# Channel attention into a GELU feed-forward: operands of v in 25 small tiles, the seven-product scheme in first steps too, softmax in ten pieces, side work placed by a table

## The chip, the cores and the metric

One core of a Trainium2 chip runs the whole program. The metric is device time in microseconds (us), the median of three runs. Engine names are those of the profile: PE (TensorE matmul), PEld (its weight load), DVE (VectorE), ACT (ScalarE), POOL (GpSimd), SP (SyncE, which issues all DMAs here).

## The reference

```
B, N, C = 4, 6080, 256          # attention over channels, per batch
qn = q / (norm(q, axis=1) + 1e-6);  kn = k / (norm(k, axis=1) + 1e-6)
s  = kn.T @ qn / tau            # 256 x 256 per batch
a  = exp(s - s.max(-1)); a /= a.sum(-1) + 1e-9
x  = v @ a                      # 6080 x 256 per batch
h  = x @ w_in                   # 256 -> 2048
out = (0.5 * h * (1 + erf(h / sqrt(2)))) @ w_out      # 2048 -> 256
```

All is float32.

## The kernel before

The product `a @ w_in` is folded once per batch into weights `wh`/`wl` (function `w_part`, four groups g of 512 hidden columns), so a token needs two products: v with these weights, then the GELU with `w_out`. Every float32 operand stands as a high part and a low part, and a product is three matmuls (`passes`: high·high, high·low, low·high).

The tokens of a batch are cut into six pairs p of blocks (twice 512 tokens, the last twice 480), each pair into eight steps u of 256 hidden units. A step (b, p, u) has *first products* (v by weights) and *second products* (GELU by `w_out`); the second products of a step are issued between the first products of the next one. Both are done by a scheme of seven products for a 2 x 2 block product instead of eight (`strassen`): the first products from the second pair of batch 0 on, the second ones from its third pair on, except in step u=0 of each pair and in the very last step. Where the second products take the scheme, the GELU goes into a tile `x` (`whole`), DVE makes sums of its blocks (`sums`, four pieces), ACT casts their high parts (`gh0`, `gh1`), DVE subtracts for the low parts (`gl0`, `gl1`), and PE runs four products of 512 columns (j=1) and seven of 256 (`work`) into the PSUM banks c00, c01, p0 and p1. Without the scheme PE runs eight of 512. At the end of a pair, `combine` and `merge` put p0, p1, c00 and c01 together on DVE and store.

The first products use two PSUM banks by turns, h0 and h1 (`ring`). The results of the first two products and of the third are copied out by ACT (p1, p5, u2), and three results are added to these by DVE (the operations written `h<-h,u2`, `h<-h,p5`, `h<-h,p1`), so that a bank comes free when its copy or addition ends.

The seven operands of v come from four blocks of a pair, loaded as one tile `v_raw`, four sums `vs0` to `vs3` (`v_sum`), and a high and low part of each (`v_split`: ACT casts `vh`, DVE subtracts `vl`). Each of these names has one buffer, so the split for the next pair overwrites the operand that the last step still reads.

Side work for the next batch runs beside the steps: scores as bursts of matmuls (`burst`; `load_qk` and `split_qk` bring their operands), sums of squares (`norm_part`), the softmax (`softmax`, a generator that is advanced in pieces), and the new weights (`load_win`, `w_part`, `w_split`). `at(step, slot, job)` puts a job into a step: slots 0 to 5 stand behind the first to sixth first product, 6 behind the last second product, 8 and 9 at the end of the step. From pair (0, 1) on every engine works in the order in which the program was written (`InOrder`); before that a scheduler orders the instructions. All records of PE, DVE and ACT carry the line of the helper, L138.

Of the kernel before, what the change touches and what calls it, by code (L numbers as in the profile page):

```python
# [17 lines left out]
P = 128  # L18
# [20 lines left out]

NS = 1024  # L40
# [9 lines left out]
NARROWS = (12, 18)  # L50

# [14 lines left out]
def channel_attention_gelu_ffn(ctx, tc, qk, kqt, vt, tau, w_in, w_out, out):  # L66
# [79 lines left out]

    raws = {}
# [39 lines left out]
    def qk_fill():  # L187
# [9 lines left out]
        acc = state["sacc"] = pm.tile([P, NCT, NT], F32, name="sacc")  # L197
# [21 lines left out]
    def burst(b, k, m):  # L219
# [121 lines left out]
    def softmax(first):  # L341
# [39 lines left out]
        dve.reciprocal(out=r, in_=z)  # L381

# [12 lines left out]
        es = []  # L395
        rden = pm.tile([P, 8], F32, name="rden", bufs=2)
# [5 lines left out]
        if not first:  # L402
            yield
# [11 lines left out]
        eh = pm.tile([P, NCT, C], F32R, name="eh")  # L415
        el = pm.tile([P, NCT, C], F32R, name="el")
# [13 lines left out]
    def w_first(g, m, tmp):  # L430

        if m == 0:
            name = (f"vh{T2}", f"vl{T2}", f"vh{T3}", f"vl{T3}")[g]
            a21s[g] = pv.tile([P, 2, 2, P], F32R, name=name)
# [19 lines left out]
    def w_part(b, g, m):  # L454
# [56 lines left out]
    def v_blocks(b, p):  # L511
        n = PAIRS[p][1]
        raw = vraw[b, p]
        return {(k, j): raw[:, k, j * n:(j + 1) * n] for k in range(2) for j in range(2)}

    def v_sum(b, p, i):
        n = PAIRS[p][1]
        x = v_blocks(b, p)
        if i == 0:
            vts[b, p] = [pv.tile([P, NT], F32, name=f"vs{k}") for k in range(4)]  # L520
        ts = [t[:, :n] for t in vts[b, p]]
        to, x0, x1 = ((0, x[0, 1], x[0, 0]), (2, x[1, 1], x[0, 1]), (1, x[1, 1], ts[0]), (3, x[1, 0], ts[1]))[i]
        dve.tensor_tensor(out=ts[to], in0=x0, in1=x1, op=ALU.subtract)

    def v_split(b, p, i):
        n = PAIRS[p][1]
        x = v_blocks(b, p)
        src = {B11: x[0, 0], B21: x[1, 0], B22: x[1, 1]}.get(i)
        if (b, p) == (0, 0) and i == B12:
            src = x[0, 1]  # L530
        if src is None:
            src = vts[b, p][i - T1][:, :n]
# [4 lines left out]
        yield  # L537
        dve.tensor_tensor(out=lo[:, :n], in0=src, in1=f32(hi[:, :n]), op=ALU.subtract)


# [14 lines left out]
    def strassen(b, p, u):  # L555
        return u > 0 and (b, p) > (0, 1) and (b, p, u) != (B - 1, NP - 1, NU - 1)
# [54 lines left out]
    def first_products(b, p, u):  # L611
# [51 lines left out]
    def plain_products(b, p, u):  # L663
# [9 lines left out]
        for j in (1, 0):  # L673
            for i in (1, 0):
# [7 lines left out]
                flush()  # L682
                if (i, j) != (0, 0):
# [4 lines left out]
    def second_products(b, p, u, blocks):  # L688
# [89 lines left out]
    def merge(b, p, c):  # L778
# [4 lines left out]
        parts = ((0, n // 2), (n // 2, n)) if last and c == NCT - 1 else ((0, n),)  # L783
        for lo, hi in parts:
# [128 lines left out]
    bursts = {}  # L913
    for b in range(1, B):
        start, num, den = (8, 5, 2) if b == 1 else (4, 14, 5)
        for k in range(FIRSTB if b == 1 else 0, NQS // NB):
            bursts[b, k] = (b - 1) * NP * NU + start + k * num // den
# [14 lines left out]
    EDGE = 8  # L932

    for (b, k), s in bursts.items():
        prev = bursts.get((b, k - 1), s - 3)
        for t in range(NB):
            js = k * NB + t
            at(prev - 1 + t, EDGE, lambda b=b, js=js: load_qk(b, js))

            def split(b=b, js=js, step=prev + 1 + t):  # L940
                gen = split_qk(b, js)
                next(gen)
                at(step, 2, lambda: next(gen, None))
            at(prev + 1 + t, 1, split)
        for m in range(NCT):
            at(s + m, EDGE, lambda b=b, k=k, m=m: burst(b, k, m))

        def drop(b=b, k=k):
            for t in range(NB):
                hls.pop((b, k * NB + t))  # L950
        at(s + 1, EDGE, drop)
    for b in range(1, B):
        base = (b - 1) * NP * NU
        for i in range(2 * NCT * NSC):

            def norm(b=b, i=i, step=base + 8 + i):
# [3 lines left out]
                at(step + 1, 2, lambda: next(gen, None))  # L960
            at(base + 8 + i, EDGE, norm)

# [110 lines left out]
```

## Time and profile before

| | |
|---|---|
| median of 3 runs | 2174.79 us (2174.49 to 2175.36) |
| profiled execution | 2174.69 us, its span 2172.9 us |
| PE busy | 2152.8 us, 99% of the span, 11061 matmuls |
| DVE busy | 1734.9 us, 80% |
| ACT busy | 1622.5 us, 75% |
| DMA | 352.18 MB, mean 162 GB/s |

Busy times are unions of the recorded durations of an engine's instructions. Durations of neighbouring matmuls overlap, so the time that one costs is the distance between starts. In a row of the timeline the text in brackets is the idle time of the engine ahead of the instruction and what ended it.

### The profile page before, as it was taken

How to read it: one execution, taken by the hardware profiler on the slowest of the kernel's cores; microseconds unless marked ns; L12 is line 12 of the kernel's file. 1: busy time of each engine (PE TensorE's matmuls, PEld its weight loads, DVE VectorE, ACT ScalarE, POOL GpSimd, SP SyncE). 2: the span in 40 equal slices, each digit the busy share in tenths (PEclk: the TensorE clock that was granted, in tenths of full speed). 3: DMA queues.
4: the chain of work that ended last, by engine and by line, in shares of the span. 5: the costliest groups of instructions: out<-in, count | busy, mean ns of one | idle time of the engine just before them, and what ended most of it. 6: DMA issues, size and time to landing. Idle time of an engine off the chain costs nothing.

```text
span 2172.9 us, 29906 instructions
## 1 busy us (share of the span) xinstructions
PE 2152.8 (99%) x11061; PEld 1822.7 (84%) x11061; DVE 1734.9 (80%) x2732; ACT 1622.5 (75%) x2692; POOL 1.3 (0%) x8
## 2 busy tenths in 40 slices
PE   9999999999999999999999999999999999999999
PEld 8777888887888888888888888888888888888888
DVE  6997788877788788887788878888778777777776
ACT  5767778867777787786777778887677777677675
POOL 0000000000000000000000000000000000000000
PEclk9999999999999999999999999999999999999999
DMA  9545655544344555553434545554344333333332
GB/s 381 180 150 199 213 184 199 183 161 146 136 144 145 176 204 180 199 202 128 140 135 141 173 168 202 184 205 163 106 146 144 118 129 114 127 128 115 125 119 95
DMA packets 100547, 352.18 MB, mean 162 GB/s; under 512 B 10288, under 2 KB 12464, under 8 KB 98352
## 3 DMA queue, kind: packets, MB, share of 16 engines
q1 hardware_dynamic: 100400, 350.27, 46.3%
q8 instruction: 87, 1.43, 0.3%
q14 instruction: 60, 0.49, 0.1%
HBM read 312.74 MB, written 37.49 MB: 161 GB/s over the span
## 4 chain that ended last, share of the span: by engine, by line
PE 87%; DVE 7%; ACT 4%; issue 1%; DMA 0%; DVEq 0%; ACTq 0%; POOL 0%; POOLq 0%
PE h L138 45%; PE c L138 33%; PE p L138 9%; DVE h L138 2%; DVE vl L138 2%; DVE x L138 1%; ACT gh L138 1%; DVE gl L138 1%; ACT x L138 1%; ACT vh L138 1%; ACT g L138 0%; DVE small L138 0%; ACT L138 0%; ACT p L138 0%; DVE osb L138 0%
## 5 line engine op out<-in xcount | busy, mean ns | idle before, releaser
L138 PE MATMUL c<-gh,wo 128*128 128x512 f32 (+3 forms) x2460 | 870.4, 364 | 0.4 <-DVE wo L138 0.4
L138 PE MATMUL h<-vh,wh 128*128 128x512 f32 (+1 forms) x1312 | 520.3, 397 | 12.9 <-DVE h L138 2.8
L138 PEld LDWEIGHTS c<-gh,wo 128*128 128x128 f32 x2460 | 462.2, 188 | 81.9 <-DVE wo L138 1.5
L138 PE MATMUL h<-vh,wl 128*128 128x512 f32 (+1 forms) x1312 | 513.5, 391 | 0.0
L138 PE MATMUL h<-vl,wh 128*128 128x512 f32 (+1 forms) x1312 | 513.5, 391 | 0.0
L138 ACT ACTIVATE gh<-h 128x512 fp32r<-128x512 f32 (+1 forms) x446 | 277.9, 623 | 238.2 <-DVE h L138 219.2
L138 PE MATMUL c<-gl,wo 128*128 128x512 f32 (+3 forms) x1230 | 443.8, 361 | 0.1
L138 DVE TENSOR_TENSOR gl<-x,gh 128x768 fp32r<-128x768 f32 (+3 forms) x306 | 329.8, 1078 | 63.5 <-ACT gh L138 63.3
L138 DVE TENSOR_TENSOR gl<-g,gh 128x512 fp32r<-128x512 f32 (+1 forms) x462 | 314.5, 681 | 49.3 <-ACT g L138 47.1
L138 DVE TENSOR_TENSOR h<-h,p 128x512 f32<-128x512 f32 (+1 forms) x368 | 251.4, 683 | 79.5 <-PE h L138 68.3
L138 ACT COPY p<-h 128x512 f32<-128x512 f32 (+1 forms) x368 | 213.7, 581 | 126.3 <-PE h L138 126.2
L138 PEld LDWEIGHTS h<-vh,wh 128*128 128x128 f32 x1312 | 247.0, 188 | 72.3 <-ACT p L138 9.2
L138 ACT CAST gh<-x 128x768 fp32r<-128x768 f32 (+3 forms) x306 | 286.8, 937 | 16.7 <-DVE x L138 11.7
L138 PEld LDWEIGHTS h<-vh,wl 128*128 128x128 f32 x1312 | 246.4, 188 | 51.9
L138 DVE TENSOR_TENSOR x<-x 128x256 f32<-128x256 f32 (+4 forms) x491 | 241.1, 494 | 52.5 <-ACT x L138 34.8
L138 PEld LDWEIGHTS h<-vl,wh 128*128 128x128 f32 x1312 | 246.7, 188 | 35.4
L138 ACT ACTIVATE g<-h 128x512 f32<-128x512 f32 (+1 forms) x446 | 271.6, 609 | 0.0
L138 PEld LDWEIGHTS c<-gl,wo 128*128 128x128 f32 x1230 | 231.0, 188 | 45.3 <-DVE gl L138 0.5
L138 ACT ACTIVATE x<-h 128x512 f32<-128x512 f32 (+1 forms) x306 | 182.3, 609 | 48.9 <-DVE h L138 47.8
L138 PE MATMUL p<-gh,ws 128*128 128x256 f32 (+1 forms) x918 | 210.2, 280 | 0.0
L138 DVE TENSOR_TENSOR h<-h,u 128x512 f32<-128x512 f32 (+1 forms) x184 | 125.8, 684 | 83.5 <-PE h L138 82.6
L138 PEld LDWEIGHTS p<-gh,ws 128*128 128x128 f32 x918 | 162.6, 189 | 6.8
(153 smaller groups left out, 2229.5 us busy)
## 6 DMA issues: line engine op xcount, KB each, us to landing
wo<-keep_out SPq DMA_DIRECT2D x184, 512.0 KB, 4.5
ws<-keep_sum SPq DMA_DIRECT2D x153, 512.0 KB, 3.7
raw<-qk SPq DMA_DIRECT2D x94, 512.0 KB, 4.5
raw<-kqt SPq DMA_DIRECT2D x72, 512.0 KB, 4.6
v_raw<-vt SPq DMA_DIRECT2D x20, 1024.0 KB, 5.0
out<-osb SPq DMA_DIRECT2D x40, 512.0 KB, 3.9
hl<-keep_in SPq DMA_DIRECT2D x12, 1024.0 KB, 5.4
raw<-w_in SPq DMA_DIRECT2D x8, 512.0 KB, 6.9
```

The source lines that it names most:

```text
L138: r = op(*args, **kw)
```

## The change

- `v` lies in 25 equal tiles v0 to v24 of 512 columns. `take` gives the one that has been free longest, `give` returns a tile at its last use in program order: a raw block or sum when its split is written, an operand when the last step's product has read it. A pair is loaded as four tiles with four DMAs. `eh`, `el` of the first softmax and the plain pair's `a21` come from the same 25; later `eh`, `el` take the buffer of `sacc`.
- The splits of the next pair stand in steps 5, 6, 7 of a pair and in the first step of the next, in place of 7 and the first; the sums in steps 1, 2, 3 and 5 in place of 3 to 6.
- `strassen` holds at u=0 too. The seven products of 256 columns go in another order, p0 first and c00 after p1. `combine` starts at the end of a pair's following first step and `merge` comes in slot 3 of the second one; where all eight steps take the scheme, half of c01 is not written, and the second merge covers half.
- The later softmaxes are advanced in ten pieces, from slot 3 of step 36 of the batch to slot 7 of step 39 (before: seven pieces, from the end of step 36 to the end of step 38), with both scalings ahead of both maxima, and the load of the exponential's table asked for at the end of step 37.
- Steps and slots of all side work come from the table `PLAN`. The bursts of batches 1 to 3 stay 10 or 12; the last `w_split` of a batch comes two steps later.

```diff
+PLAN = {
...
+    "soft": (3, 10, 11, 16, 17, 18, 21, 22, 26, 37),
...
+    "vhi": (52, 54, 66, 71, 72, 73, 81),
+    "vlo": (63, 70, 71, 73, 75, 80, 82),
...
+    room = deque(range(NV))
+    def take(count, dtype=F32R, shape=(P, NT)):
+        got = []
+        for _ in range(count):
+            i = room.popleft()
+            t = pv.tile(list(shape), dtype, name=f"v{i}")
+            owner[id(t)] = i, t
+            got.append(t)
+        return got
+    def give(*tiles):
+        for t in tiles:
+            room.append(owner.pop(id(t))[0])
...
         for m in range(NCT):
             dve.scalar_tensor_tensor(out=ts[m], in0=ts[m], scalar=rk[:, m:m + 1], in1=rq[:, 0:C],
                                            op0=ALU.mult, op1=ALU.mult)
+        if not first:
+            yield
+        for m in range(NCT):
             dve.reduce_max(out=nms[:, m:m + 1], in_=ts[m], axis=AX.X, negate=True)
         yield
         es = []
+        if not first:
+            preload(AF.Exp, x)
+            yield
...
-        raw = pv.tile([P, NCT, 2 * NT], F32, name="v_raw")
-        nc.sync.dma_start(out=raw[:, :, :2 * n],
-                          in_=vt[:, b * N + t0:b * N + t0 + 2 * n].rearrange("(t p) n -> p t n", p=P))
+        raw = {}
+        for k, j in ((0, 0), (1, 0), (1, 1), (0, 1)):
+            x, = take(1, F32)
+            t = b * N + t0 + j * n
+            nc.sync.dma_start(out=x[:, :n], in_=vt[k * P:(k + 1) * P, t:t + n])
+            raw[k, j] = x
...
-        hi = pv.tile([P, NT], F32R, name=f"vh{i}")
-        lo = pv.tile([P, NT], F32R, name=f"vl{i}")
+        hi, = take(1)
+        act.copy(out=hi[:, :n], in_=src[:, :n])
+        yield
+        lo, = take(1)
         vops[b, p, i] = hi, lo
-        act.copy(out=hi[:, :n], in_=src)
-        yield
-        dve.tensor_tensor(out=lo[:, :n], in0=src, in1=f32(hi[:, :n]), op=ALU.subtract)
+        dve.tensor_tensor(out=lo[:, :n], in0=src[:, :n], in1=f32(hi[:, :n]), op=ALU.subtract)
+        give(src)
...
-        return u > 0 and (b, p) > (0, 1) and (b, p, u) != (B - 1, NP - 1, NU - 1)
+        return (b, p) > (0, 1) and (b, p, u) != (B - 1, NP - 1, NU - 1)
...
             product(b, p, u, *ORDER[i], ps, start, stop)
+            if u == NU - 1:
+                give(*vops.pop((b, p, ORDER[i][1])))
...
-        work = (("c00", 1, wpair(0, 0), hb, lb, 2), ("p0", 0, wpair(0, 1), hb, lb, 0),
-                ("c00", 0, (ws[:, 0, 3], ws[:, 1, 3]), hb, lb, 1), ("p1", 0, (ws[:, 0, 0], ws[:, 1, 0]), ht, lt, 0),
-                ("p1", 1, (ws[:, 0, 2], ws[:, 1, 2]), ht, lt, 1), ("p0", 1, (ws[:, 0, 1], ws[:, 1, 1]), ht, lt, 2),
+        work = (("p0", 0, wpair(0, 1), hb, lb, 0), ("p0", 1, (ws[:, 0, 1], ws[:, 1, 1]), ht, lt, 2),
+                ("p1", 0, (ws[:, 0, 0], ws[:, 1, 0]), ht, lt, 0), ("p1", 1, (ws[:, 0, 2], ws[:, 1, 2]), ht, lt, 1),
+                ("c00", 1, wpair(0, 0), hb, lb, 2), ("c00", 0, (ws[:, 0, 3], ws[:, 1, 3]), hb, lb, 1),
                 ("c01", 1, wpair(1, 0), ht, lt, 3))
...
+        if c == NCT - 1 and all(strassen(b, p, u) for u in range(NU)):
+            parts = ((n // 2, n),)
...
-                        spread(gen, step, 1)
+                        spread(gen, step, PLAN["end"][1])
```

The order of instructions at three places. First DVE from the end of step u=0 into u=1 in batch 3, third pair (osb is the pair's output tile, x the GELU tile). Before:

```order
L138 TENSOR_TENSOR gl1_18909<-g_18910,gh1_18908 128x512
L138 TENSOR_TENSOR gl0_18924<-g_18925,gh0_18923 128x512
L138 TENSOR_TENSOR osb_18952<-p0_18271,osb_18952 128x256
L138 TENSOR_TENSOR osb_18952<-p1_18286,osb_18952 128x256
L138 TENSOR_TENSOR osb_18952<-osb_18952,p1_18286 128x256 x2
L138 TENSOR_TENSOR osb_18952<-c00_18175,osb_18952 128x512
L138 TENSOR_TENSOR osb_18952<-c01_18187,osb_18952 128x512
L138 TENSOR_TENSOR h_18982<-h0_18956,u2_18971 128x512
```

After, the same place on DVE:

```order
L171 TENSOR_TENSOR x_19273<-x_19273 128x512
L171 TENSOR_TENSOR x_19273<-x_19273 128x256
L171 TENSOR_TENSOR osb_19305<-p0_18531,osb_19305 128x256
L171 TENSOR_TENSOR osb_19305<-p1_18546,osb_19305 128x256
L171 TENSOR_TENSOR x_19273<-x_19273 128x256
L171 TENSOR_TENSOR gl1_19295<-x_19273,gh1_19294 128x768
L171 TENSOR_TENSOR osb_19305<-osb_19305,p1_18546 128x256 x2
L171 TENSOR_TENSOR gl0_19297<-x_19273,gh0_19296 128x1024
L171 TENSOR_TENSOR h_19354<-h0_19332,u2_19346 128x512
L171 TENSOR_TENSOR osb_19305<-c00_18559,osb_19305 128x512
L171 TENSOR_TENSOR osb_19305<-c01_18566,osb_19305 128x256
```

The sums of x and two wider subtractions take the place of two of 512 columns, the combine operations stand between them, and the merges moved behind the add h.

Second, ACT in step u=0 of the same pair, before (p1, p5, u2 are the copies that free the banks):

```order
L138 COPY p1_18834<-h0_18830 128x512
L138 CAST gh0_18822<-x_18792 128x1024
L138 CAST vh1_18841<-v_raw_18212 128x512
L138 COPY p5_18849<-h1_18845 128x512
L138 CAST vh6_18855<-vs3_18404 128x512
L138 COPY u2_18862<-h0_18830 128x512
```

And after, on ACT:

```order
L171 COPY p1_19202<-h0_19198 128x512
L171 CAST gh0_19188<-x_19163 128x1024
L171 COPY p5_19215<-h1_19211 128x512
L171 CAST v6_19221<-v2_18779 128x512
L171 COPY u2_19226<-h0_19198 128x512
```

One cast of v left this step, and the other one stands behind the copy p5.

Third, ACT at the exponentials of batch 2's softmax, in the fifth pair (t0, t1 are the scores; the table load ahead of gh is the GELU's). Before:

```order
L138 COPY p1_16012<-h1_16008 128x512
L138 CAST gh0_15992<-x_15968 128x1024
L138 COPY p5_16023<-h0_16019 128x512
L138 COPY u2_16032<-h1_16008 128x512
L138 ACT_TABLE_LOAD
L138 ACTIVATE t0_15882,small_15881<-t0_15882,small_15881 128x256
L138 ACTIVATE t1_15884,small_15881<-t1_15884,small_15881 128x256
L138 ACT_TABLE_LOAD
L138 ACTIVATE gh_16045<-h_16043 128x512
```

After, on ACT:

```order
L171 CAST gh1_16306<-x_16279 128x768
L171 ACT_TABLE_LOAD
L171 ACTIVATE junk_16317<-small_16131 128x2
L171 COPY p1_16324<-h1_16320 128x512
L171 CAST gh0_16308<-x_16279 128x1024
L171 COPY p5_16335<-h0_16331 128x512
L171 ACTIVATE t0_16132,small_16131<-t0_16132,small_16131 128x256
L171 COPY u2_16346<-h1_16320 128x512
L171 ACTIVATE t1_16134,small_16131<-t1_16134,small_16131 128x256
L171 ACT_TABLE_LOAD
L171 ACTIVATE gh_16357<-h_16355 128x512
```

The first table load moved to the end of the step before, and the exponentials stand on either side of the copy u2.

More of the change, by code (lines that the diff above doesn't have):

```diff
@@ L38 @@
 NB = 2
+NV = 25
 NS = 1024
@@ L50 @@
 NARROWS = (12, 18)
+PLAN = {
+    "first": {
+        "splits": (10, 10, 13, 14, 15, 16, 18, 19, 20, 21, 23, 24, 25, 26, 28, 29, 30, 31, 33, 34),
+        "loads": (8, 8, 11, 12, 13, 14, 16, 17, 18, 19, 21, 22, 23, 24, 26, 27, 28, 30, 31, 32),
+        "bursts": ((12, 13), (14, 15), (17, 18), (19, 20), (22, 23), (24, 25), (27, 28), (29, 30), (32, 33), (34, 35)),
+        "norms": (9, 10, 11, 12, 13, 14, 15, 16, 17, 19, 20, 21, 22, 23, 25, 26, 27, 28, 29, 30, 31, 32, 33, 34),
+    },
+    "later": {
+        "splits": (2, 3, 5, 6, 7, 8, 10, 11, 13, 14, 16, 17, 19, 20, 21, 22, 24, 26, 27, 28, 30, 31, 33, 34),
+        "loads": (0, 1, 3, 4, 5, 6, 8, 9, 11, 12, 14, 15, 17, 18, 19, 20, 22, 24, 25, 26, 28, 29, 31, 32),
+        "bursts": ((3, 5), (6, 7), (9, 10), (11, 12), (15, 16), (17, 18), (20, 21), (24, 25), (26, 27), (28, 30), (32, 33), (34, 35)),
+        "norms": (2, 3, 4, 5, 6, 7, 9, 10, 11, 12, 13, 14, 16, 17, 18, 19, 20, 21, 22, 23, 25, 26, 27, 29),
+    },
+    "burst": 8,
+    "part": 8,
+    "square": 2,
+    "qhi": 1,
+    "qlo": 2,
+    "start": 36,
+    "soft": (3, 10, 11, 16, 17, 18, 21, 22, 26, 37),
+    "win": (39, 40, 43, 45),
+    "wpart": (41, 43, 45, 47),
+    "wsplit": (42, 44, 46, 50),
+    "wslots": (10, 12, 13, 18, 22, 26),
+    "vload": 0,
+    "vsum": (17, 27, 38, 53),
+    "vhi": (52, 54, 66, 71, 72, 73, 81),
+    "vlo": (63, 70, 71, 73, 75, 80, 82),
+    "end": (8, 10, 13, 13),
+}
 GAPS = (7, 4, 2)
@@ L395, in softmax @@
         es = []
+        if not first:
+            preload(AF.Exp, x)
+            yield
         rden = pm.tile([P, 8], F32, name="rden", bufs=2)
@@ L401, in softmax @@
             es.append(e)
-        if not first:
-            yield
+            if not first:
+                yield
         for m in range(NCT):
@@ L414, in softmax @@
                    identity=ident)
[L415 to L416 removed]
+        if first:
+            eh, el = state["eh"] = take(2)
+        else:
+            keep = pm.tile([P, 2, NT], F32R, name="sacc")
+            eh, el = keep[:, 0], keep[:, 1]
+        eh, el = (x.rearrange("p (d c) -> p d c", d=NCT) for x in (eh, el))
         marks["eh"] = act.copy(out=eh, in_=tpv)
@@ L516, in v_sum @@
     def v_sum(b, p, i):
         n = PAIRS[p][1]
[L518 to L523, printed above, removed]
+        x = vraw[b, p]
+        ts = vts.setdefault((b, p), {})
+        to, x0, x1 = ((T1, x[0, 1], x[0, 0]), (T2, x[1, 1], ts.get(T1)), (T4, x[1, 0], ts.get(T2)),
+                      (T3, x[1, 1], x[0, 1]))[i]
@@ L682, in plain_products @@
                 flush()
+                if u % 2 == 1 and (i, j) == (0, 0):
+                    give(a21)
+                if u == NU - 1 and i == 0:
+                    for x in cols[j]:
+                        give(*vops.pop((b, p, x)))
                 if (i, j) != (0, 0):
@@ L912, in channel_attention_gelu_ffn, with base_soft, plan @@
     FIRSTB = FILL // NB
[L913 to L917, printed above, removed]
+    def base_soft(b):
+        return (b - 1) * NP * NU + PLAN["start"]
+    def plan(b):
+        p = PLAN["first" if b == 1 else "later"]
+        return p["loads"], p["splits"], p["bursts"]
     jobs = {}
@@ L930, in spread, with split, drop, norm @@
             at(step + x // 10, x % 10, lambda: next(gen, None))
[L932 to L951, printed above, removed]
+    EARLY, EDGE = 7, 8
     for b in range(1, B):
         base = (b - 1) * NP * NU
-        for i in range(2 * NCT * NSC):
-            def norm(b=b, i=i, step=base + 8 + i):
+        loads, splits, bursts = plan(b)
+        for k in range(FIRSTB if b == 1 else 0, NQS // NB):
+            r = k - (FIRSTB if b == 1 else 0)
+            for t in range(NB):
+                js = k * NB + t
+                at(base + loads[NB * r + t], EDGE, lambda b=b, js=js: load_qk(b, js))
+                def split(b=b, js=js, step=base + splits[NB * r + t]):
+                    gen = split_qk(b, js)
+                    next(gen)
+                    at(step, PLAN["qlo"], lambda: next(gen, None))
+                at(base + splits[NB * r + t], PLAN["qhi"], split)
+            for m in range(NCT):
+                at(base + bursts[r][m], PLAN["burst"], lambda b=b, k=k, m=m: burst(b, k, m))
+            def drop(b=b, k=k):
+                for t in range(NB):
+                    hls.pop((b, k * NB + t))
+            at(base + bursts[r][1], EDGE + 1, drop)
+        for i, x in enumerate(PLAN["first" if b == 1 else "later"]["norms"]):
+            def norm(b=b, i=i, step=base + x):
                 gen = norm_part(b, *divmod(i, NSC))
```

70 lines of the change are left out of this document (36 added, 34 removed).

## The prediction

> **What bounds the kernel now.** I read the page's busy times first, then the chain, then PE's timeline for the spacing of its matmuls, then windows cut at the starts of steps. On the page (busy share of each engine, the granted clock in 40 slices, the chain's shares):
>
> ```profile
> span 2172.9 us, 29906 instructions
> PE 2152.8 (99%) x11061; PEld 1822.7 (84%) x11061; DVE 1734.9 (80%) x2732; ACT 1622.5 (75%) x2692; POOL 1.3 (0%) x8
> PEclk9999999999999999999999999999999999999999
> PE 87%; DVE 7%; ACT 4%; issue 1%; DMA 0%; DVEq 0%; ACTq 0%; POOL 0%; POOLq 0%
> ```
>
> PE is busy for 99% of the span at full clock and carries 87% of the chain; DMA carries none of it. So a change can win in two ways: fewer matmul columns, or fewer of the gaps in which PE waits for DVE and ACT. The price of a column comes from PE's timeline in an undisturbed step (start, duration, operands):
>
> ```profile
> 1302.84 0.39 PE L138 MATMUL h<-vh,wh 128*128 128x512 f32 x1
> ...
> 1303.53 0.28 PE L138 MATMUL c<-gh,wo 128*128 128x256 f32 x1
> ...
> 1304.23 0.40 PE L138 MATMUL h<-vh,wh 128*128 128x512 f32 x1
> ```
>
> Three 512-column matmuls start within 0.69 us, the six 256-column ones behind them within 0.70. So a trio (the three passes of one product) costs 0.69 us at 512 columns and 0.35 at 256; the printed durations overlap and are no price.
>
> Windows cut at step starts (stretch, length, then busy time of PE, PEld, DVE, ACT, POOL): a plain step of batch 3, a step with a burst, a step u=1, the three softmax steps (u=5 to 7 of the fifth pair) of batches 0 and 2, and u=0 to 2 at the start of batches 1 and 3:
>
> ```profile
> 1872.73:1882.82 10.09, 10.09 (x57) 8.66 (x55) 7.51 (x12) 7.00 (x12) 0.00 (x0) 1.00 0.31 106
> 1352.58:1364.06 11.48, 11.48 (x64) 9.88 (x63) 9.32 (x13) 8.87 (x14) 0.00 (x0) 1.00 0.55 190
> 1852.21:1862.64 10.43, 10.43 (x47) 8.37 (x46) 8.11 (x14) 7.11 (x13) 0.00 (x0) 1.00 0.52 177
> 481.90:517.29 35.39, 32.54 (x170) 26.67 (x169) 28.40 (x60) 25.16 (x43) 0.00 (x0) 1.00 0.24 87
> 1554.19:1589.63 35.44, 32.56 (x171) 26.68 (x169) 28.60 (x61) 25.77 (x44) 0.00 (x0) 1.00 0.25 90
> 604.14:637.70 33.56, 32.95 (x160) 26.68 (x160) 29.48 (x47) 25.80 (x44) 0.00 (x0) 1.00 0.43 151
> 1676.47:1709.73 33.26, 32.66 (x161) 26.68 (x161) 28.45 (x47) 25.46 (x44) 0.00 (x0) 1.00 0.39 139
> ```
>
> The same view over the 19 steps u=0 that follow another pair of their batch (first, last and sum of 19):
>
> ```profile
> 1318.89:1330.63 11.74, 11.74 (x65) 9.77 (x63) 10.69 (x16) 10.90 (x19) 0.00 (x0) 1.00 0.72 250
> ...
> 1841.69:1852.21 10.52, 10.38 (x57) 8.59 (x56) 9.65 (x15) 9.31 (x17) 0.00 (x0) 1.00 0.67 226
> sum 210.84, PE 208.56 PEld 172.50 DVE 191.81 ACT 189.44 POOL 0.00; mean PE 10.98 PEld 9.08 DVE 10.10 ACT 9.97 POOL 0.00
> ```
>
> A plain step has 11 trios of 512 and 7 of 256: 7.59 + 2.45 = 10.04, measured 10.09; a burst adds 1.39. So plain steps hold no wait. From that the waits follow:
> - u=0: seven of the 19 steps are plain in matmuls (10.09), seven hold a burst (11.48), four have products of 480 columns (21 matmuls shorter by 32/512 of 230 ns: 9.79), one has whole second products, 15 trios and a burst (11.76): 201.9 in all. Measured 210.84, so **8.9 us** waited.
> - softmax: three plain steps and six small matmuls (0.7 at 117 ns each) are 31.0; 35.4 measured; **13.3 us** in three batches.
> - batch starts: steps of 9.8 (second products of 480 columns), 10.4 (15 trios) and 10.1, and one w_part group of six matmuls (1.38), are 31.7; measured 33.56, the same in batch 2, and 33.26, so **5.4 us**.
> - u=1: 10.43 against 10.09 is mostly the work counted next; of waiting it holds 0.04 to 0.1, some 1.9 us over 19 steps at most.
>
> **The change part by part.**
>
> *Scheme in the first steps.* At u=0 the four 512-column trios of group j=0 (2.76 us) become seven of 256 (2.46). The 10.43 us step above is where those second products run, and it exceeds the plain step by 0.34, 0.04 of that a wait. 22 pairs, the four of 480 columns a little less: **−6.4 us**. This is work on the bound engine, so nothing can hide it or take it back but a wait. Its other side is on DVE and ACT, by these rows (operation, count, busy, mean ns):
>
> ```profile
> L138 DVE TENSOR_TENSOR gl<-g,gh 128x512 fp32r<-128x512 f32 x388 | 266.0, 686 | 43.1 <-ACT g L138 41.2 <-PE c L138 0.7
> L138 DVE TENSOR_TENSOR gl<-x,gh 128x1024 fp32r<-128x1024 f32 x126 | 154.3, 1225 | 33.8 <-ACT gh L138 33.8
> L138 DVE TENSOR_TENSOR gl<-x,gh 128x768 fp32r<-128x768 f32 x126 | 119.9, 952 | 0.0
> L138 DVE TENSOR_TENSOR x<-x 128x256 f32<-128x256 f32 x252 | 106.4, 422 | 6.4
> L138 DVE TENSOR_TENSOR x<-x 128x512 f32<-128x512 f32 x126 | 87.0, 691 | 34.6 <-ACT x L138 26.4
> L138 ACT ACTIVATE gh<-h 128x512 fp32r<-128x512 f32 x372 | 233.2, 627 | 185.6 <-DVE h L138 170.7 <-PE c L138 13.2
> L138 ACT ACTIVATE x<-h 128x512 f32<-128x512 f32 x252 | 151.6, 613 | 42.2 <-DVE h L138 41.8
> L138 ACT CAST gh<-x 128x1024 fp32r<-128x1024 f32 x126 | 132.6, 1053 | 12.5 <-DVE x L138 11.7
> L138 ACT CAST gh<-x 128x768 fp32r<-128x768 f32 x126 | 105.7, 839 | 3.4
> ```
>
> DVE drops two gl (1.37) and gains 0.69 + 2×0.42 + 0.95 + 1.22 = 3.71: +2.3 us a pair. ACT drops four gelus (2.5) and gains two (1.23) and two casts (1.89): +0.6. The cover is the slack in the step that follows, u=1, where the previous pair's combine and merges now stand among these. In PE's order there, product k of the seven starts at 1.38(k−1) us up to the fifth. DVE starts its sums 0.61 after the seventh product of u=0, which three 256-column trios (1.05) follow, so at −0.44. Its chain to the next add h is 0.69 + 0.42 + two combine ops of 256 columns (0.84) + 0.42 + 0.95 + two more (0.84) + 1.22 = 5.38: it ends at 4.94. The add can begin when the fourth product ends, at 4.83, and takes 0.69: done at 5.63. PE wants that bank for the sixth product at 4.83 + 0.69 + 0.69 + 0.70 = 6.91. So 1.3 us of slack, more where a burst lies ahead: I cost it at **0**, and the 0.1 us a boundary that I leave below covers small misses. The dropped half of the last merge takes 0.27 off DVE. Seconds are reordered so that p0 comes first and c00 after its merge; the lo half of the later blocks is wanted at 6.7, and its producer ends at 4.94.
>
> The 22 extra ws loads and the v loads in four parts add DMA issues on SP, which the chain does not contain:
>
> ```profile
> ws<-keep_sum SPq DMA_DIRECT2D x153, 512.0 KB, 3.7
> ```
>
> A load of 3.7 us has more than a step before its use. The tiles that the v loads overwrite were last read by the fourth and fifth products of the step before, so SP does not block ws or wo behind them: 0.
>
> *Splits spread over u=5 to 8.* The wait at u=0 in the timeline (batch 3; ACT, then the weight load that waited):
>
> ```profile
> 1844.99 0.62 ACT L138 CAST vh<-v_raw 128x512 fp32r<-128x512 f32 x1
> 1845.51 0.58 ACT L138 COPY p<-h 128x512 f32<-128x512 f32 x1
> 1846.15 0.19 PEld L138 LDWEIGHTS h<-vh,wh 128*128 128x128 f32 x1 [0.57 <-ACT p L138]
> ```
>
> A cast of v stands ahead of the copy that frees the bank. The change puts that cast behind the copy, and of seven casts two stand in u=5, one in u=6, three in u=7 and one in u=0 (before: five and two); DVE loses one subtraction at u=0 and reaches its add h 0.69 earlier. I let 1.9 of the 8.9 stay (0.1 each): **−7.0**. u=1 keeps its 1.9.
>
> *Softmax in ten pieces.* The first rows are DVE's, the others ACT's, of batch 0's softmax:
>
> ```profile
> 486.34 0.16 DVE L138 TENSOR_SCALAR small<-small 128x4 int32<-128x4 int32 x1
> ...
> 489.04 0.68 DVE L138 TENSOR_TENSOR h<-h,u 128x512 f32<-128x512 f32 x1
> ...
> 498.90 1.28 ACT L138 ACT_TABLE_LOAD   x1
> 500.20 0.51 ACT L138 ACTIVATE t<-t,small 128x256 f32<-128x256 f32 x1
> ...
> 501.31 1.28 ACT L138 ACT_TABLE_LOAD   x1
> 502.61 0.63 ACT L138 ACTIVATE gh<-h 128x512 fp32r<-128x512 f32 x1
> ```
>
> 2.7 us of small DVE operations stand in front of an add that PE needs, and two table loads with two exponentials (3.7 us) in front of a gelu. After the change the sums of t no longer precede the small operations (two of 0.42 and two small ones, moved to the step before), and these stand ahead of gl0, whose cast DVE used to wait for. From −0.44: sums and gl1 2.48, small ones 2.2, gl0 1.22, diag 0.65, add 0.69: done at 6.8 against 6.91, no wait but no slack. One table load lies under the first product. What stays late: the softmax's four 256-column operations (1.8) now stand ahead of the sums, which end at about 2.9 instead of 1.1; the 1.05 cast follows, then the p5 copy (0.58), at 4.5, where the fourth product wants its bank at 4.14. I take 0.4 for this and 0.6 for the banks of the transposes and of the row sums: 1.0 left a batch, **−10.3**. ACT's second table load is still ahead of a gelu, but that gelu's result is wanted only in the next step.
>
> The Trainium skill (ScalarE: Activation LUTs, What ACT_TABLE_LOAD costs) puts 1283 ns for the load and 1380 for a drain, some 2.66 us for a switch. The trace agrees on the load and shows no drain: the exponential begins 0.02 us after the load's end. By the page the two switches would hold ACT 2.8 us longer in each of three softmaxes, and the sum below would be at most 8 us higher.
>
> *Batch starts.* The last w_split moves two steps later, out of the step that also ends a pair: I let 0.6 of 1.8 stay, **−3.6**. *Pairs 0 and 1* wait some 4 us by the same count (an estimate from plain steps); DVE has the same operations there in another order: **−1** (bounds −2 and +1). *Start:* the first softmax now does both scalings before both maxima, so the first exponential comes up to 0.42 later (a 256-column operation): **+0.3** (bounds 0 and 0.5).
>
> Sum: −6.4 − 7.0 − 10.3 − 3.6 − 1 + 0.3 = −28.0. The profiled execution took 2174.69 us (1.8 beyond its span) and the median of the runs is 2174.79, so the forecast is **2147 us**.
>
> **Rivals.**
> 1. *The waits change places.* The slack of 1.3 us at u=1 is worked out with row means, the softmax's copy is 0.4 late already, and DVE in u=7 and u=0 still has bursts, splits and norms. If half of the 21.9 us of waits that the sum takes away return elsewhere, and each of 22 boundaries waits 0.2 us more, the time is 2146.7 + 11 + 4.4 = 2162. For it: DVE 10.69 of 11.74 us busy in the u=0 row. Against: the after-order has less in that step.
> 2. *DVE becomes the bound at each pair's second step* (the slower side). The 2.3 us of sums and 2.8 of combine and merges share one step. If DVE cannot use its 1.3 us of slack because its inputs come one after the other (combine waits for ACT's copy, gl0 for a cast that waits for the third sum), PE waits for the add. It decides from 1.3 us of wait a boundary (28.0/22); at 2.3, the whole addition uncovered, 2174.7 − 28.0 + 22×2.3 = 2197. Against: bursts of 9.32 us DVE in 11.48 run without any wait.
> 3. *The tiles do not decouple.* If splits wait for tiles that the running step frees, u=0 keeps its 8.9 and the batch starts their 5.4, and the late splits cost as much again at u=1: 2174.7 − 6.4 − 10.3 + 14.3 = 2172. Against: each split takes tiles that an earlier product freed.
> 4. *Narrow matmuls cost more than half.* If each 256-column matmul waited out its 188 ns weight load, a u=0 would cost 21×0.188 = 3.95 against 2.76, 22×1.2 = 26 us more, and the sum would be 2174.7 − 21.6 + 26 = 2179. The rows above (0.70 us for six) exclude nearly all of it.
>
> The Trainium skill (TensorE: Matmul & The Clock Gate, Back-to-back issue gap) gives 131 ns sustained for 512 columns and 81 for 128 in streams of load and matmul; an estimate between them is 98 for 256, by which 21 halves (2.06) cost more than 12 wholes (1.57), and the first term would be +11 us. The trace disagrees: 230 and 117 ns.
>
> **How the numbers follow.** Forecast 0.72 (2138 to 2155: from all the waits counted gone, another 8.5 us, to 8 us less gain), rival 1 0.16, rival 2 0.05, rival 3 0.06, rival 4 0.01. The range 2138 to 2163 takes in the forecast and more than half of rival 1. What a measurement of this kernel can tell is about 0.2%, 4.3 us: forecast and rival 1 are faster, rival 3 is within it or a little faster, rivals 2 and 4 are slower or, in their milder half, level with before: 0.90, 0.05, 0.05.
>
> **What the profile after would show.** Step u=1 at 10.09 us in batch 3 and u=0 at 10.1 to 10.2: the first two terms. Softmax steps in 32 us instead of 35.4. Batch starts within 32 us. A weight load at u=1 that waits for the add h, or u=1 above 10.5, is rival 1 or 2; waits of v casts for PE, or of ws loads, rival 3. The prediction is wrong if the second steps of pairs get longer than they were.

## The result, and the profile after

The changed kernel takes **2142.26 us** (median of six runs, 2141.63 to 2142.51), the kernel before 2174.77 beside it (2174.36 to 2175.36): −32.5 us, ratio 0.985 with a 95% interval of 0.9837 to 0.9862. The profiled execution took 2142.28 us. On the page of the changed kernel (span, busy times, granted clock, chain):

```profile
span 2140.4 us, 30621 instructions
PE 2131.2 (100%) x11259; PEld 1828.8 (85%) x11259; DVE 1768.9 (83%) x2798; ACT 1634.7 (76%) x2695; POOL 1.3 (0%) x8
PEclk9999999999999999999999999999999999999999
PE 92%; DVE 0%; DMA 0%; issue 0%; ACT 0%; DVEq 0%; ACTq 0%
```

DVE and ACT stand at 0% of the chain (7% and 4% before), although both do more work than before. (This chain could be followed back only to 140.9 us of the span, so its shares add up to 93% and leave out the first pair; the one of the kernel before reaches the start.) Windows cut at step starts (stretch, length, then busy time of PE, PEld, DVE, ACT, POOL): a plain step, a u=0 with a burst, a u=1, the softmax of batches 0 and 2, the starts of batches 1 and 3; then the sum of the 19 steps u=0 that stood in the prediction's second view:

```profile
1831.88:1841.97 10.09, 10.09 (x56) 8.66 (x55) 7.51 (x12) 7.00 (x12) 0.00 (x0) 1.00 0.29 106
1298.82:1310.30 11.48, 11.48 (x65) 9.89 (x63) 10.26 (x15) 9.99 (x17) 0.00 (x0) 1.00 0.63 219
1821.78:1831.88 10.10, 10.10 (x56) 8.66 (x55) 9.67 (x18) 7.13 (x13) 0.00 (x0) 1.00 0.44 157
480.83:512.34 31.51, 31.51 (x170) 26.48 (x169) 27.87 (x58) 27.13 (x48) 0.00 (x0) 1.00 0.39 134
1531.56:1563.08 31.52, 31.52 (x170) 26.49 (x169) 27.89 (x58) 27.13 (x48) 0.00 (x0) 1.00 0.39 134
598.36:629.74 31.38, 31.38 (x169) 26.92 (x168) 27.64 (x43) 25.18 (x42) 0.00 (x0) 1.00 0.45 163
1649.08:1680.47 31.39, 31.39 (x169) 26.91 (x168) 26.45 (x42) 23.28 (x39) 0.00 (x0) 1.00 0.36 130
...
sum 202.07, PE 202.07 PEld 174.27 DVE 177.67 ACT 164.56 POOL 0.00; mean PE 10.64 PEld 9.17 DVE 9.35 ACT 8.66 POOL 0.00
```

PE's busy time now equals the length in every one of them: the first steps went from 210.84 to 202.07 us, a softmax from 35.4 to 31.5, a batch start from 33.5 to 31.4, and u=1 from 10.43 to 10.10, the length of a plain step.

Below, PE's waits are counted from its timeline in one way for all kernels: by how much the distance between the starts of two neighbouring matmuls exceeds the undisturbed one (231 ns at 512 columns, 117.5 at 256, 216 at 480, 111.5 at 240; the few other shapes by their own). Over the whole span they fall from 38.4 us to 13.2, and the undisturbed distances themselves add up to 2128.6 before and 2122.1 after. The kernel before ran at 2174.8 to 2175.7 us in the five groups of runs behind this text, so a difference of less than 1 us between kernels of different groups tells nothing.

### The profile page after: what moved, and what is told of

It reads as the page before. It is cut to its first block, busy times and chain, and to the rows that moved or that the text cites. A ratio compares the mean times of both kernels' runs of the same rounds, so it can differ in the third digit from the quotient of the medians.

```text
span 2140.4 us, 30621 instructions
## 1 busy us (share of the span) xinstructions
PE 2131.2 (100%) x11259; PEld 1828.8 (85%) x11259; DVE 1768.9 (83%) x2798; ACT 1634.7 (76%) x2695; POOL 1.3 (0%) x8
## 4 chain that ended last, share of the span: by engine, by line
PE 92%; DVE 0%; DMA 0%; issue 0%; ACT 0%; DVEq 0%; ACTq 0%
PE h L171 47%; PE c L171 33%; PE p L171 12%; DMA wo<-keep_out 0%; DVE x L171 0%; DVE osb L171 0%; DVE hl L171 0%; DVE h L171 0%; ACT g L171 0%; ACT gh L171 0%; DVE v L171 0%; DVE gl L171 0%; DVEq L1143 0%; ACT osb L171 0%; ACTq L171 0%
## 5 line engine op out<-in xcount | busy, mean ns | idle before, releaser
L171 PE MATMUL c<-gh,wo 128*128 128x512 f32 (+3 forms) x2372 | 827.9, 359 | 0.6 <-DVE wo L171 0.6
L171 PE MATMUL h<-v,wh 128*128 128x512 f32 (+1 forms) x2624 | 814.4, 391 | 1.1 <-DVE h L171 1.1
L171 PEld LDWEIGHTS h<-v,wh 128*128 128x128 f32 x2624 | 455.4, 188 | 73.4 <-ACT p L171 2.2
L171 PE MATMUL h<-v,wl 128*128 128x512 f32 (+1 forms) x1312 | 513.4, 391 | 0.0
L171 DVE TENSOR_TENSOR gl<-x,gh 128x768 fp32r<-128x768 f32 (+1 forms) x350 | 376.6, 1076 | 57.4 <-ACT gh L171 57.4
L171 ACT CAST gh<-x 128x768 fp32r<-128x768 f32 (+1 forms) x350 | 327.9, 937 | 46.2 <-DVE x L171 26.9
L171 DVE TENSOR_TENSOR x<-x 128x256 f32<-128x256 f32 (+2 forms) x557 | 274.4, 495 | 80.5 <-ACT x L171 67.5
L171 PEld LDWEIGHTS h<-v,wl 128*128 128x128 f32 x1312 | 246.4, 188 | 52.1
L171 DVE TENSOR_TENSOR h<-h,p 128x512 f32<-128x512 f32 (+1 forms) x368 | 250.8, 682 | 47.7 <-PE h L171 35.4
L171 DVE TENSOR_TENSOR v<-v,v 128x512 fp32r<-128x512 f32 (+3 forms) x257 | 173.9, 677 | 0.5 <-ACT v L171 0.5
L171 PE MATMUL p<-gl,ws 128*128 128x256 f32 (+1 forms) x525 | 146.5, 279 | 0.0
```

Of the source, the lines that this page charges most:

```text
L171: r = op(*args, **kw)
```

## The experiments

### How much room DVE has in the second step

The step u=1 of batch 3 after the change, ACT, DVE and PE (start, duration; in brackets the idle time ahead and what ended it):

```profile
1824.14 1.05 ACT L171 CAST gh<-x 128x1024 fp32r<-128x1024 f32 x1 [0.86 <-DVE x L171]
1825.10 0.57 ACT L171 COPY p<-h 128x512 f32<-128x512 f32 x1
...
1821.56 1.15 DVE L171 TENSOR_TENSOR x<-x 128x512 f32<-128x512 f32 x2 [0.75 <-ACT x L171]
1822.82 0.95 DVE L171 TENSOR_TENSOR osb<-p,osb 128x256 f32<-128x256 f32 x2
1823.69 0.41 DVE L171 TENSOR_TENSOR x<-x 128x256 f32<-128x256 f32 x1
...
1826.90 0.69 DVE L171 TENSOR_TENSOR h<-h,u 128x512 f32<-128x512 f32 x1
...
1825.93 0.63 PE L171 MATMUL h<-v,wh 128*128 128x512 f32 x2
...
1828.72 0.63 PE L171 MATMUL h<-v,wh 128*128 128x512 f32 x2
```

The third add h of the step (`h<-h,u`) ends at 1827.59 and PE wants its bank at 1828.72: 1.1 us of room. But there is a second chain: combine's additions (osb) stand ahead of the third sum of x, ACT's cast waits 0.86 us for that sum, and the copy of the second product stands behind the cast. It ends at 1825.67, and PE takes its bank at 1825.93. To see which of the two sets the time, DVE got three more operations ahead of both:

```diff
+        for _ in range(3 if state.get('u0') else 0):
             tt(out=x[:, 4 * h:6 * h]..., in0=x[:, h:3 * h]..., in1=x[:, 0:h]..., op=ALU.subtract)
```

> The changed kernel with three more 512-column sums on DVE (a repeat of the first sum of x) at the end of each pair's first step, 21 pairs: a test of how much room DVE has in the second step. By the traces the three take 1.8 to 2.1 us, and the slack measured after the change is 1.0 to 1.1 us. Theory (that slack is all there is): PE waits some 0.8 to 1.0 us a pair, 2142.3 + 17 to 22 = 2159 to 2164 us. Rival A (no slack, DVE sets the time there): 21 x 1.9 = 40 us, 2182 us. Rival B (the slack is larger than read, since late work is taken up by later steps): under 5 us, below 2147 us.

Measured 2180.84 us (2178.36 to 2181.68): +38.6, by its size rival A (22 steps carry the sums, not 21). The step in batch 3, and ACT and the weight load in it:

```profile
1853.65:1865.63 11.98, 10.38 (x57) 8.58 (x55) 11.66 (x21) 7.14 (x13) 0.00 (x0) 1.00 0.37 131
...
1857.98 1.04 ACT L171 CAST gh<-x 128x1024 fp32r<-128x1024 f32 x1 [2.84 <-DVE x L171]
1858.93 0.58 ACT L171 COPY p<-h 128x512 f32<-128x512 f32 x1
...
1859.56 0.30 PEld L171 LDWEIGHTS h<-v,wh 128*128 128x128 f32 x2 [2.03 <-ACT p L171]
```

The cast starts 4.33 us after the step's start instead of 2.36, so 1.97 later, and PE waits 1.77 for the copy: the room was **0.2 us**, in ACT's queue and not at the add. The copy's own input was there: the second product starts 1.4 us into the step and takes 0.7. The copy stood behind a cast that waited. The Trainium skill (PSUM — Partial Sum Buffer, Engine vs sequencer instructions) says that the queues of ScalarE and VectorE are strict FIFO; the trace agrees, by these 2.84 us. In 14 of the 22 steps PE waits for this copy (24.2 us in all); in the other eight, which all follow a burst, it waits for DVE's addition of the burst's scores (9.0 us), which the extra sums hold up as well.

Next, combine was moved behind the third sum, with the three sums kept:

```diff
-    "end": (8, 10, 13, 13),
+    "end": (10, 11, 13, 13),
```

> The kernel of the three extra sums, with combine starting one slot later, behind the third of the sums of x and the first low part instead of between them (slots 10, 11, 13, 13). In the extra sums' trace PE waits 1.77 us a pair for the copy of the second product, and that copy stands behind a cast that waits for the third sum, ahead of which combine's first two additions (0.86 us from start to start) stand. Theory (that chain, sum to cast to copy to bank, is what binds; the third add h, with 1.1 us of room, does not yet): the copy comes 0.86 us earlier, PE waits 0.9 a pair, so 2180.8 - 21 x 0.86 = 2163 us. Rival (DVE's total of work in that step binds, whatever its order): it stays at 2180 us.

Measured 2179.72 us: the rival is right. The 1.1 us between the two medians are not to the order's credit: in the profile of the run before, the granted clock is 0.50 in two stretches of 3.4 us (from 264.0 and 1247.1 us), where matmuls of 512 columns start 427 ns apart and PE loses 3.1 us. Without these, PE's waits in the second steps are 36.1 us in that profile and 36.4 in this one. In the step of batch 3 the cast came 0.74 us earlier, but combine's copy moved in between:

```profile
1852.93:1864.61 11.68, 10.54 (x57) 8.69 (x56) 10.94 (x20) 6.56 (x12) 0.00 (x0) 1.00 0.37 135
...
1857.48 0.37 ACT L171 COPY osb<-p 128x256 f32<-128x256 f32 x1
1857.74 0.59 ACT L171 COPY p<-h 128x512 f32<-128x512 f32 x1
```

That gave 0.3 a step. In six steps u=1 with a burst and a splitting it cost 0.6: the wait of 1.0 to 1.2 us for the burst's addition stays, and another of 0.5 comes at the third add h. DVE is nearly full there already without the extra sums, as this window of the changed kernel shows (fourth pair of batch 0):

```profile
347.25:358.73 11.48, 11.48 (x65) 9.89 (x64) 11.20 (x19) 8.86 (x14) 0.00 (x0) 1.00 0.62 214
```

So in these burst steps DVE has hardly any time left (11.20 of 11.48 us busy), and in the others the room is what ACT's queue leaves.

### The scheme in the first steps

The scheme alone, put into the kernel before:

```diff
-        return u > 0 and (b, p) > (0, 1) and (b, p, u) != (B - 1, NP - 1, NU - 1)
+        return (b, p) > (0, 1) and (b, p, u) != (B - 1, NP - 1, NU - 1)
...
+        if c == NCT - 1 and all(strassen(b, p, u) for u in range(NU)):
+            parts = ((n // 2, n),)
```

> The kernel before with one thing alone, the scheme in the first step of each pair too (and the half as long last addition that goes with it); large tiles, places and softmax stay. Theory (the parts add up): 2174.8 - 6.4 = 2168.4 us. Rival (the first step is where DVE is late already, with 8.7 us of PE's waits; the added sums make it later and eat the gain): 2173 to 2180 us.

Measured 2189.95 us (before: 2175.71), ratio 1.0066 (1.0054 to 1.0079): slower by 14.2. PE's waits in the steps u=1 rose from 1.9 to 17.9 us, those at the batch starts from 5.4 to 10.8. The rival is right, and more than it asked (2180 at most): alone, the scheme brings about 20 us of waits and saves 6.4. Of the waits in u=1, 8.9 us stand at the third add h and 7.4 at the first product into c00, whose bank a merge on DVE frees.

The reverse, the scheme taken out of the changed kernel (the first line of the diff turned round):

> The changed kernel, but the first step of each of the 22 pairs of columns computes its products the plain way again (eight second products, no sums). Theory (the scheme is worth its shorter PE time and nothing else, since the waits of these steps are already gone): the changed kernel's 2142.3 plus 22 x 0.29 = 6.4, so 2148.7 us, with PE's waits as they are. Rival (the sums that the scheme adds on DVE load the boundary between pairs, so leaving them out relieves it): part of the 6.4 comes back, 2145 or less; but waits in these steps are already nearly nil, so it should not.

Measured 2173.34 us, +31.1, outside both expectations. PE waits 15.6 us in the steps u=1, 5.4 in the steps u=0 and 3.3 at the batch starts (next to nothing with the scheme). Around the start of one step u=1, at 1846.81, ACT and PE:

```profile
1846.70 0.63 ACT L171 ACTIVATE gh<-h 128x512 fp32r<-128x512 f32 x1 [1.69 <-PE c L171]
1847.24 0.61 ACT L171 ACTIVATE g<-h 128x512 f32<-128x512 f32 x1
1847.76 0.58 ACT L171 ACTIVATE gh<-h 128x512 fp32r<-128x512 f32 x1
1848.24 0.59 ACT L171 ACTIVATE g<-h 128x512 f32<-128x512 f32 x1
...
1848.88 0.72 PE L171 MATMUL h<-v,wh 128*128 128x512 f32 x2 [0.52 <-ACT g L171]
1854.15 0.47 PE L171 MATMUL c<-gh,wo 128*128 128x512 f32 x1 [0.16 <-DVE osb L171]
```

A plain first step writes its last GELUs into the tiles gh1 and gh0, and the products of the step before into c00, which the new order puts near the end, still read gh1. So ACT waits 1.69 us for a product into c, four gelu operations are left to the next step, and the bank that the last of them reads comes free late: 14.1 us of PE's waits stand there. Another 5.9 stand at c00, which without the scheme is wanted as fifth second product, right behind the merges in slot 3. Whether the new order is to blame was tested by undoing both together (old `work`, `"end": (10, 11, 12, 12)`):

> The changed kernel without the scheme in first steps, and with the old order at the end of a pair as well, so that the two are undone together. Theory (the 25 us of waits that came when the scheme alone was taken out are the new order's, which fits only a step with seven narrow products: with the scheme c00 is wanted as ninth product, without it as fifth): those waits go, 2142.3 + 6.4 + up to 2 = 2148 to 2151 us. Rival (the waits come from the scheme's absence itself, since a plain first step hands its GELU over later): it stays near 2173 us.

Measured 2149.36 us, +7.1: the theory, though by the rows above c00 was the smaller part of the waits. Its waits in u=1 are 1.1 us, and the gelu into gh1 starts 1.45 us ahead of the step u=1 instead of 0.11 (third pair of batch 3). And the other way round, scheme and new order together in the kernel before (`work` as in the change, combine from the end of the first step, merges in slot 3 of the second):

> The kernel before with the scheme in first steps and the new order at the end of a pair, large tiles and old places otherwise. Theory (scheme and order belong together, the rest adds up): 2175.7 - 6.4 = 2169 us, perhaps 2 us less since u=1 loses its waits. Rival (casts and subtractions of v still stand in u=0 and make the sums late): u=1 waits as with the scheme alone, 2180 to 2190 us.

Measured 2170.46 us (before: 2174.91), ratio 0.9979 (0.997 to 0.9988): −4.5, near the theory's −6; u=1 waits 1.35 us in place of 17.9, while the batch starts wait 2.4 more than in the kernel before. The last corner, the scheme with the old order in the changed kernel:

> The changed kernel with the end of a pair as it was: c00 first among the seven narrow products, combine from the start of the pair's following second step, both merges ahead of the third add of that step. Theory (the scheme at u=0 is free only because combine starts a step earlier, c00 comes last and the merges stand behind the add): u=1 waits again as it did where the scheme was put alone into the kernel before (19.6 us more in u=1 and the batch starts' second steps), some 2160 us. Rival (the splittings' new places alone make room on DVE): 2142 to 2146 us.

Measured 2156.43 us, +14.2, of it 14.0 of waits in the steps u=1: the theory, at some four fifths of its size. DVE in such a step, and the weight load that waits:

```profile
794.76 1.02 DVE L171 TENSOR_TENSOR osb<-c,osb 128x512 f32<-128x512 f32 x2
795.70 1.22 DVE L171 TENSOR_TENSOR hl<-raw,hl 128x1024 fp32r<-128x1024 f32 x1
796.83 0.68 DVE L171 TENSOR_TENSOR h<-h,u 128x512 f32<-128x512 f32 x1
...
797.57 0.30 PEld L171 LDWEIGHTS h<-v,wh 128*128 128x128 f32 x2 [1.30 <-DVE h L171]
```

The merges (osb from c, 1.02 us) and a splitting stand ahead of the add h. The change puts the merges behind it; the bank c00, which they free, is then wanted later, since c00 stands near the end of `work`. In the changed kernel the four corners are 2142.3 us (scheme, new order), 2156.4 (scheme, old order), 2149.4 (plain, old order) and 2173.3 (plain, new order): the scheme pays only with this order, and the order only with the scheme.

### The places of the splittings

```diff
-    "vhi": (52, 54, 66, 71, 72, 73, 81),
-    "vlo": (63, 70, 71, 73, 75, 80, 82),
+    "vhi": (71, 72, 73, 75, 76, 80, 81),
+    "vlo": (72, 73, 74, 76, 80, 81, 82),
```

> The changed kernel with its 25 small tiles of v, but with the seven splittings of v at the old places, the last two steps of a pair. Theory A (the places are what matters; the tiles only allow them): the waits of the first and second step (8.7 and 1.9 before) come back and the starts of the batches in part, 9 to 14 us, so 2151 to 2156 us. Theory B (giving tiles back one by one is what matters: a splitting no longer waits for a reader of a large tile): nothing comes back, 2142 to 2144 us.

Measured 2163.84 us, +21.6: theory A, and more than it asked. The steps u=0 wait 13.6 us (0.05 with the new places), the first steps of batches 4.0, u=1 0.9. ACT in a u=0 of batch 3, and the weight load:

```profile
1835.00 0.61 ACT L171 CAST v<-v 128x512 fp32r<-128x512 f32 x1
1835.52 0.58 ACT L171 COPY p<-h 128x512 f32<-128x512 f32 x1
...
1836.14 0.30 PEld L171 LDWEIGHTS h<-v,wh 128*128 128x128 f32 x2 [0.56 <-ACT p L171]
```

It is the picture of the kernel before, with 25 small tiles: a cast of v ahead of the copy. In the changed kernel the copy comes first and the cast after it:

```profile
1814.06 0.58 ACT L171 COPY p<-h 128x512 f32<-128x512 f32 x1
1814.54 0.62 ACT L171 CAST v<-v 128x512 fp32r<-128x512 f32 x1
```

So with the tiles and without the places the gain is gone: the places bring it. (The sums of v kept their new places here and were not undone alone.) That the tiles are needed for them follows from the program alone and was not run: with one buffer a name, a split in step 5 would overwrite an operand that steps 5 to 7 still read.

The last `w_split` of a batch back at its old place (`"wsplit": (42, 44, 46, 48)`):

> The changed kernel with the last splitting of a batch's weights back in the step in which a batch begins, two steps earlier. Theory (the prediction's: this move is what took the batch starts' 5.4 us of waits away): 4 us or so come back in three batch starts, 2146 us. Rival (the splittings of v did it: with them alone at their old places the batch starts wait 4.0 us again in their first steps): no wait comes back, 2142 to 2143 us.

Measured 2147.6 us, +5.3: the theory, a little more. But the waits come back elsewhere than they stood before: none in the first step of a batch, 2.2 us in the second, 1.5 in the third, 1.4 in the fourth. In the second step a cast of `w_split` (0.82) stands ahead of ACT's copy of the second product; in the third the subtractions of `w_split` (0.95) and of a splitting (1.22) stand ahead of the add h; in the fourth PE waits for the copy again. The waits in the first steps of batches (4.6 us before) are those of the splittings of v: 4.0 of them came back with their old places.

### The softmax

The seven pieces, places and order of before, without the early table load:

> The changed kernel with the softmax of the later batches as it was: seven pieces at the old places, the two exponentials in one piece, no early load of the tables, each row's scaling and maximum in turn. Theory (the cutting up and the places of the softmax are what took its waits away): the three softmaxes wait 13.4 us on PE again instead of 1.7, so 2142.3 + 11.7 = 2154.0 us. Rival (a part of the softmax's waits went because the sums and the splittings of v no longer fall into the same steps): only about half of it comes back, 2146 to 2150 us.

Measured 2155.57 us, +13.3: the theory. The nine softmax steps wait 14.7 us instead of 1.7. Which of the ten pieces did it: with DVE's cutting kept, and both exponentials together again without the early load,

```diff
-        if not first:
-            preload(AF.Exp, x)
-            yield
...
-            if not first:
-                yield
+        if not first:
+            yield
```

> The changed kernel with both exponentials of a softmax in one piece and without the early load of the exponential's table; the cutting up of DVE's part stays. Theory (ACT's part never made PE wait: in the trace before, PE's waits of a softmax stand at DVE's small operations, at the scalings and maxima and at the transposes, none behind the exponentials): 2142 to 2144 us. Rival (the step terms of the prediction, by which two table loads and two exponentials ahead of a gelu cost as well): 1 to 2 us a softmax, 2145 to 2148 us.

Measured 2144.53 us, +2.3: between the two, nearer the theory. The softmaxes wait 3.6 us, 0.6 each more than with ten pieces, at the end of the step:

```profile
498.60 1.28 ACT L171 ACT_TABLE_LOAD   x1
499.89 0.63 ACT L171 ACTIVATE gh<-h 128x512 fp32r<-128x512 f32 x1
...
502.42 0.30 PEld L171 LDWEIGHTS h<-v,wh 128*128 128x128 f32 x2 [0.47 <-DVE h L171]
```

So of some 4 us that a softmax gained, ACT's part is 0.6. The rest, by difference, belongs to DVE's pieces and their places, which were not undone alone: the small operations, the scalings and the end of the softmax no longer stand as a block ahead of an add.

### What is left

Two of the waits that stand in the trace of the changed kernel, DVE and PE: two splittings of scores' operands in one step of the second pair, and a subtraction behind combine in the last step.

```profile
182.10 2.35 DVE L171 TENSOR_TENSOR hl<-raw,hl 128x1024 fp32r<-128x1024 f32 x2
184.37 0.68 DVE L171 TENSOR_TENSOR h<-h,u 128x512 f32<-128x512 f32 x1
...
185.11 0.30 PEld L171 LDWEIGHTS h<-v,wh 128*128 128x128 f32 x2 [1.37 <-DVE h L171]
...
2133.34 0.72 DVE L171 TENSOR_TENSOR osb<-osb,p 128x240 f32<-128x240 f32 x2
2133.97 0.65 DVE L171 TENSOR_TENSOR gl<-g,gh 128x480 fp32r<-128x480 f32 x1
...
2134.68 0.48 PE L171 MATMUL c<-gl,wo 128*128 128x480 f32 x1 [0.82 <-DVE gl L171]
```

These and two more were to be taken away in one kernel:

```diff
-GAPS = (7, 4, 2)
+GAPS = (7, 5, 2)
...
-        "splits": (10, 10, 13, 14, 15, ...
+        "splits": (10, 11, 13, 14, 15, ...
...
+            if first:
+                dve.reduce_max(out=nms[:, m:m + 1], in_=ts[m], axis=AX.X, negate=True)
...
-            if last and name == "c01" and u < NU - 1:
+            if last and (name, half) == ("p1", 1) and u < NU - 1:
...
-                for i, x in enumerate(PLAN["vsum"]):
+                for i, x in enumerate(PLAN["vsum"] if (b, p) > (0, 0) else (36, 46, 56, 66)):
```

> The changed kernel with the waits that are left in its trace taken one by one: the first two splittings of scores' operands in steps 10 and 11 instead of both in 10 (1.1 us of wait in the third step of the second pair), combine of the last pair right behind the products of p1 (1.0 in the last step), the sums of v for the second pair in the places before (0.8 and 0.5 in the first pair), scaling and maximum of the first softmax row by row again and one matmul more ahead of its transposes (0.75). Theory (these waits are independent): 2142.3 - 3 to 4 = 2138 to 2139 us. Rival (they turn up again at the next thing late, since DVE is 99% busy in the first pair): 2140 to 2142 us.

Measured 2140.44 us (2140.19 to 2141.03), ratio to before 0.984 (0.9827 to 0.9854): 1.8 us below the changed kernel, half of what was expected, and measured in another group, so that the two intervals overlap widely; PE's waits fall from 13.2 to 11.7. The first softmax gave its 0.4 (0.755 to 0.33) and the second pair 0.8, but an add of the same pair now waits 0.76 instead of 0.33. The waits of 0.8 and 0.5 in the first pair did not move, so the sums of v were not their cause. The rows of the changed kernel show it for the first, ahead of the second:

```profile
76.11 1.22 DVE L171 TENSOR_TENSOR wl<-hl,wh 128x1024 fp32r<-128x1024 f32 x1
77.25 0.68 DVE L171 TENSOR_TENSOR hl<-osb 128x512 fp32r<-128x512 f32 x1
...
77.99 1.20 PE L171 MATMUL p<-hl,v 128*128 128x512 f32 x4 [0.65 <-DVE hl L171]
```

PE waits for the low part of `w_in` (hl), and the subtraction for the low part of the weights (wl, 1.22 us) stands ahead of it. In the kernel before the two stand the other way round, and the step waits 0.25 us there instead of 1.3. Why the scheduler, which orders the first pair, turned them stays open. In the last step of this latest kernel combine's additions still wait for ACT:

```profile
2130.14 0.92 DVE L171 TENSOR_TENSOR osb<-p,osb 128x240 f32<-128x240 f32 x2 [2.20 <-ACT osb L171]
```

ACT is late because the very last step is a plain one and meets what the run without the scheme met: its gelu into gh1 waits until c00's products have read that tile. In the changed kernel:

```profile
2130.16 0.60 ACT L171 ACTIVATE gh<-h 128x480 fp32r<-128x480 f32 x1 [1.57 <-PE c L171]
```

The last step waits 0.39 us in the kernel before and with the old order in the changed one, and 1.08 with the new order in either kernel. So its wait belongs to the order of `work`, and moving combine could not take it away (0.2 us less).

## Why the prediction was right, point by point

Waits by the count above, in us:

| step of the prediction | forecast | traces, before → after |
|---|---|---|
| scheme, narrower matmuls | −6.4 | −6.5 (2128.6 → 2122.1) |
| waits at u=0 | −7.0 | −8.65 (8.70 → 0.05) |
| waits at u=1 | 0 | −1.9 (1.90 → 0.00) |
| softmax | −10.3 | −11.7 (13.4 → 1.7) |
| batch starts | −3.6 | −5.4 (5.4 → 0) |
| pairs 0 and 1 | −1 | +0.9 (4.4 → 5.3) |
| start | +0.3 | +0.3 (0.46 → 0.76) |
| last step | not named | +0.7 (0.39 → 1.08) |
| sum | −28.0 | −32.3; runs −32.5 |

- *Scheme.* Term and size hold. No matmul costs more than half: rival 4 is out. Put alone into the kernel before, it lost 14.2 us, which the prediction did not see: it wrote the reordering off in one sentence ("p0 comes first and c00 after its merge"), and that sentence carried the term.
- *The slack at u=1.* The cost of 0 is right and its ground is wrong; that it came out is partly luck. The prediction followed DVE's chain to the add h and found 1.3 us (1.1 in the trace). It did not follow the other one, third sum, cast, copy of the second product, bank, though it did so for the softmax; that chain has 0.2 us. Rival 2 was therefore much nearer than its chance of 0.05 says: by these figures an estimated 1.5 us more of DVE work a boundary (0.2 of room and the 1.3 from which that rival decides) would have made it true, not 2.6.
- *Waits at u=0, u=1 and the batch starts.* At u=0 the mechanism was the right one (casts of v ahead of copies). At the batch starts the prediction named `w_split` alone; 4.0 of the 5.4 us came back with the old places of the splittings of v, and `w_split` at its old place brings other waits. The sizes were too small, because I let 5.6 us of waits stay for safety and 0.1 stayed: where an operation moved behind the copy that it had held up, the wait was gone, not smaller.
- *Softmax.* Right in size, but half of its stated ground hardly counts: put back into the changed kernel, the block of table loads and exponentials costs 0.6 us of waits a softmax. After the change 0.6 us a softmax stay, at the row sums and the transposes, where 1.0 was left. The gelu above starts 0.01 us after its table load ends; the drain of 1380 ns that the Trainium skill adds to the load at every switch (ScalarE: Activation LUTs, What ACT_TABLE_LOAD costs) shows in no run here, neither behind a load nor ahead of one (0.02 us from the instruction before).
- *Pairs 0 and 1, last step.* Pairs 0 and 1 came out 1.9 us off and with the wrong sign, within the stated bounds: DVE's other order there costs 1.0 in the first pair (the low part of the weights ahead of that of `w_in`) and 1.1 in the second (two splittings in one step), and saves less elsewhere. The 0.7 of the last step was not named: it is gh1, held by c00's products. This is rival 1, at 1.6 us of its 15.4.
- *Rival 3* is out: no cast of v waits for PE in the steps u=0.

## What to carry to other kernels

When work moves next to an operation that frees a buffer, follow every engine's queue to that buffer, not only the queue of the engine that got the work: the tightest chain here ran through a third engine's cast and copy. Two edits that look separate, fewer matmuls and another order of the closing additions, can each lose alone and win together; undo them singly and jointly before crediting either. When products change their order, look also at the tiles that they read: the order that freed the bank c00 in time held gh1 longer, which costs plain steps that write gh1 from a bank (0.7 us in the very last step, 14.1 in the run without the scheme). The undone parts here (scheme with its order, places of the splittings, softmax, `w_split`) cost 7.1, 21.6, 13.3 and 5.3 us, 47 in all for a gain of 32.5: the parts are not additive.
